# Denominators and pair preparation a group later, the feed-forward queued by token block, the rounding without mid waits, sums of the first batch on VectorE

## The chip, the cores and the metric

The kernel runs on 1 core of one Trainium2 chip. The metric is the device time of one execution in microseconds; the figure for the kernel before is the median of 3 runs. A profile is one further execution, in which the hardware recorded every instruction, wait and DMA. Engines: PE (TensorE: matmuls, with its weight loads listed as PEld), DVE (VectorE), ACT (ScalarE), POOL (GpSimd) and SP (SyncE, which here only issues DMAs). Each engine works through its own instructions in the order in which the program wrote them.

## The reference

Routed attention, then a bilinear feed-forward, all in float32. Batch 4, 8 heads, 768 tokens, head size 64, 16 clusters a head; 3072 tokens of 512 features, 1536 hidden features.

```python
q_assign = np.argmax(np.einsum('bhsd,hcd->bhsc', q_n, c_n), axis=-1)   # normalized q, centroids
k_assign = np.argmax(np.einsum('bhsd,hcd->bhsc', k_n, c_n), axis=-1)
mask = q_assign[:, :, :, None] == k_assign[:, :, None, :]
scores = np.where(mask, scale * np.matmul(q, k.transpose(0, 1, 3, 2)), -1000000000.0)
attn = np.exp(scores - np.max(scores, axis=-1, keepdims=True))
attn = attn / (np.sum(attn, axis=-1, keepdims=True) + 1e-09)
x = np.matmul(attn, v).transpose(0, 2, 1, 3).reshape(B * S, H * D)
out = ((x @ w_a) * (x @ w_b)) @ w_out          # weights passed as float64
```

## The kernel before

The order of instructions on each engine is the order of the program text; nothing is reordered by a scheduler.

*Units, groups, pairs.* Heads are taken in 16 pairs p (4 per batch). A unit is 128 keys (index j, 0 to 5) against half the queries (384, index hf) for both heads of a pair (index a). Two units make a group, 6 groups (GPP) a pair, 96 groups (NG) in all. The main loop (L527) goes over groups g; p, l = divmod(g, 6). The three groups with l = 0, 1, 2 are the first half of a pair's queries, l = 3, 4, 5 the second.

*One turn of the loop.* `score` of group g: 4 one-hot matmuls (L371) put a large negative number where clusters differ, 4 score matmuls (L380) add on top, into one of 2 PSUM buffers `s` per unit, and ScalarE takes the exponentials into `pt` (L387; 4 buffers, two groups). Then `add_up` of group g - 1 (L400): sums of the probabilities over j, elementwise, into `acc`; for a = 1 and for j = 2 and 4 on GpSimd, else on VectorE. Then `weigh` of group g - 1 (L411): probabilities times v into `O`; after the last j ScalarE copies `O` to `xT` (L419). Then one step of the next pair's preparation, then roundings that are due, then feed-forward pieces, then `denominators` and `normalize` where they fall.

*Preparation* of pair p + 1 (`prep_steps`, L343): l=0 transposes of q and k, first third (L275); l=1 the other two thirds and the DMAs of the pair after; l=2 similarities to the centroids (L288) and the DMA of v; l=3 `prep_assign`: transposes (L299) and five VectorE passes that turn maxima into one-hots (L305 to L316); l=5 transposes of the one-hots (L326) and two ScalarE copies (L331, L333).

*Denominators.* At g % 3 == 0 ones are multiplied with `acc` (L427), ScalarE copies the result to `den` and sums it into `stat` (L431). At g % 3 == 1 `normalize` takes three reciprocals on VectorE (L440), GpSimd multiplies `xT` by them (L442), and ScalarE makes a pass over `den` that fills another column of `stat` (L444).

*Feed-forward.* A batch has two blocks of 384 tokens. A block is 24 up pieces (w_a and w_b in turn for 12 slices of hidden features, L458; ScalarE copies the first to `ha`, L469, VectorE multiplies the second into `h`, L473) and 3 down pieces (L479), whose result ScalarE copies to `y` (L483), which SP stores. Pieces wait in the queue `ffn`; a turn may spend PER_GROUP = 4608 columns, an up piece costs 1536 and a down piece 6144. A batch's pieces are queued when its last half is normalized. What is left after the loop runs at the end, behind one piece and a matmul (L572) that checks all denominators; a second path, which runs only if that check fails, is not entered.

*Weights* arrive as float64 in 36 parts of 128x512 (`load_w`, 512 KB each, 2 buffers `raw`) and are rounded to float32 from their bits (`round_w`): on VectorE L222, L225, L229, L232, and L235, which takes the exponent; a sum on GpSimd (L238); and a VectorE pass that sets the tiniest to zero (L240). `due` (L514) gives the group in which a part is rounded: 2, 5, ..., 23 for the first eight, then 1.6 a group from 24. The DMA of part i + 2 follows the rounding of part i on SP.

*Buffers.* PSUM: `s` 2, `O` 1, and 3 buffers `m` for everything else: transposes, similarities, one-hots, denominators, feed-forward pieces. The kernel opens with the centroids' norms on ScalarE and VectorE (L83 to L105) and the whole preparation of pair 0 (L519 to L526).

## Time and profile before

| | us |
|---|---|
| median of 3 runs | 1224.48 (1223.28 to 1226.19) |
| the profiled execution, its own time | 1223.04 |
| its span, first to last instruction | 1221.3 |
| PE busy | 1162.9 |
| DVE / ACT / POOL busy | 413.5 / 317.8 / 326.0 |
| granted TensorE clock, mean | 0.983 |
| first score matmul | 18.1 |
| group 24 (pair 4) begins | 144.6 |
| first feed-forward piece | 160.5 |
| last sums of attention | 1002 |
| last feed-forward matmul ends | 1216 |

The span is what the profile covers, from the first to the last instruction; the run's own time is 1.7 us longer. A busy share is an average over stages, so it is read by stretches. A wait is named by the instruction that waited and by the one that released it; a line number stands for all instructions that one line of the program issues. Slices of the page are 30.5 us each.

### The profile page before, as it was taken

Reading aid. Unit: us, or ns where it says so; the run is one execution under the profiler, and the core shown is the slowest. Engines: PE = TensorE matmul, PEld = TensorE weight load, DVE = VectorE, ACT = ScalarE, POOL = GpSimd, SP = SyncE. Lnnn points to the kernel's source line nnn. Section 1 sums busy time; section 2 is a strip of 40 time slices with the busy share of each in tenths; the row PEclk is TensorE's granted clock in tenths of the full one; section 3 lists DMA queues with packets and bytes.
Section 4 is the critical chain, followed back from the end, with each engine's and each line's share of the span. In section 5 each row is a group of like instructions: output and inputs, shape, how many; then the busy total and the mean of one; then the engine's idle time right before and its main releaser. Section 6 shows DMA issues by size and latency. Waiting matters only on the chain.

```text
span 1221.3 us, 11866 instructions
## 1 busy us (share of the span) xinstructions
PE 1162.9 (95%) x4723; PEld 576.6 (47%) x4723; DVE 413.5 (34%) x602; ACT 317.8 (26%) x575; POOL 326.0 (27%) x301
## 2 busy tenths in 40 slices
PE   6978869999989999999999999999999998999998
PEld 3333335545544445554455544554445544554553
DVE  3777777677671202223112321313022221100100
ACT  4544422222322223322223223222233211000000
POOL 2665643344432212222112222204122220000000
PEclk8998979999999999999999999999999999999999
DMA  4212241412311001010010102010000000000000
GB/s 117 76 56 72 74 125 53 125 52 83 94 35 35 31 18 48 1 39 9 27 31 1 39 13 53 1 39 1 18 22 1 1 9 17 1 1 26 1 1 28
DMA packets 63374, 44.91 MB, mean 37 GB/s; under 512 B 51536, under 2 KB 55632, under 8 KB 63312
## 3 DMA queue, kind: packets, MB, share of 16 engines
q1 hardware_dynamic: 63168, 44.05, 12.6%
q8 instruction: 39, 0.64, 0.2%
q14 instruction: 23, 0.19, 0.1%
q10 hardware_dynamic: 144, 0.03, 0.0%
HBM read 37.78 MB, written 6.29 MB: 36 GB/s over the span
## 4 chain that ended last, share of the span: by engine, by line
PE 80%; DVE 8%; issue 5%; POOL 5%; ACT 1%; DMA 0%; POOLq 0%; DVEq 0%; ACTq 0%
PE m L458 37%; PE m L479 20%; PE O L411 8%; PE s L380 7%; PE s L371 2%; POOL acc L400 2%; DVE den L440 2%; PE m L427 2%; PE m L275 2%; DVE acc L400 2%; POOL wb_sb L238 1%; POOL wa_sb L238 1%; PE m L288 1%; POOL wo_sb L238 1%; DVE rest L232 1%
## 5 line engine op out<-in xcount | busy, mean ns | idle before, releaser
L458 PE MATMUL m<-xT,wa_sb 128*128 128x384 f32 x768 | 268.3, 493 | 13.9 <-ACT sim L293 10.7
L458 PE MATMUL m<-xT,wb_sb 128*128 128x384 f32 x768 | 267.6, 492 | 2.1 <-DVE h L473 2.1
L479 PE MATMUL m<-wo_sb,h 128*128 128x512 f32 x576 | 251.5, 594 | 0.0
L400 POOL TENSOR_TENSOR acc<-acc,pt 128x384 f32<-128x384 f32 x192 | 204.4, 1080 | 52.4 <-ACT pt L387 47.4
L458 PEld LDWEIGHTS m<-xT,wa_sb 128*128 128x128 f32 x768 | 144.9, 192 | 123.5 <-ACT sim L293 11.3
L458 PEld LDWEIGHTS m<-xT,wb_sb 128*128 128x128 f32 x768 | 145.3, 192 | 100.2 <-issue 3.5
L473 DVE TENSOR_TENSOR h<-ha,m 128x384 f32<-128x384 f32 x96 | 52.7, 552 | 368.8 <-PE m L458 368.8
L479 PEld LDWEIGHTS m<-wo_sb,h 128*128 128x128 f32 x576 | 108.0, 190 | 133.5 <-issue 130.6
L387 ACT ACTIVATE pt<-s 128x768 f32<-128x768 f32 x192 | 145.1, 806 | 64.1 <-PE s L380 60.6
L411 PE MATMUL O<-pt,v 128*64 128x384 f32 x768 | 145.8, 501 | 0.0
L469 ACT COPY ha<-m 128x384 f32<-128x384 f32 x96 | 46.0, 480 | 377.7 <-PE m L458 377.5
L380 PE MATMUL s<-qkT 64*128 64x384 f32 x768 | 143.9, 495 | 0.0
L400 POOL TENSOR_TENSOR acc<-pt 128x384 f32<-128x384 f32 x32 | 39.5, 1235 | 353.0 <-PE m L427 333.4
L400 DVE TENSOR_TENSOR acc<-acc,pt 128x384 f32<-128x384 f32 x64 | 74.1, 1157 | 126.7 <-POOL acc L400 126.7
L440 DVE RECIPROCAL den<-den 128x128 f32<-128x128 f32 x96 | 82.3, 913 | 23.4 <-ACT den L431 22.8
L411 PEld LDWEIGHTS O<-pt,v 128*64 128x64 f32 x768 | 46.9, 137 | 88.4 <-issue 87.8
L380 PEld LDWEIGHTS s<-qkT 64*128 64x128 f32 x768 | 72.7, 193 | 33.2 <-issue 3.0
L442 POOL TENSOR_TENSOR xT<-xT,den 128x384 f32<-128x384 f32 x32 | 31.9, 997 | 190.2 <-DVE den L440 188.3
L483 ACT COPY y<-m 128x512 f32<-128x512 f32 x24 | 14.1, 586 | 244.6 <-PE m L479 244.6
L400 DVE TENSOR_TENSOR acc<-pt 128x384 f32<-128x384 f32 x32 | 18.6, 580 | 142.0 <-PE m L427 135.1
L371 PE MATMUL s<-ohT 64*128 64x384 bf16 x384 | 49.3, 336 | 8.8 <-ACT ohT L333 8.8
L427 PE MATMUL m<-acc,ones 128*64 128x384 f32 x128 | 35.5, 528 | 12.2 <-DVE acc L400 12.2
(77 smaller groups left out, 507.2 us busy)
## 6 DMA issues: line engine op xcount, KB each, us to landing
qk<-in_q_dram SPq DMA_DIRECT2D x32, 192.0 KB, 3.6
qk<-in_k_dram SPq DMA_DIRECT2D x32, 192.0 KB, 3.9
v<-in_v_dram SPq DMA_DIRECT2D x16, 384.0 KB, 4.4
raw<-in_moe_w_a_dram SPq DMA_DIRECT2D x12, 512.0 KB, 3.6
raw<-in_moe_w_b_dram SPq DMA_DIRECT2D x12, 512.0 KB, 3.6
raw<-in_moe_w_out_dram SPq DMA_DIRECT2D x12, 512.0 KB, 3.3
out_dram<-y SPq DMA_DIRECT2D x24, 256.0 KB, 2.0
csb<-in_centroids_dram ACTq DMA_DIRECT2D x1, 32.0 KB, 1.8
```

Source lines behind the costliest of these rows:

```text
L238: nc.gpsimd.tensor_tensor(out=w, in0=w, in1=rest, op=ALU.add)
L371: nc.tensor.matmul(out=s[:, a, 0:HB], lhsT=ohTs[p][r, S + j * P:S + (j + 1) * P], rhs=ohTs[p][r, hf * HB:(hf + 1) * HB], start=True, stop= ...
L380: nc.tensor.matmul(out=s[:, a, 0:HB], lhsT=qkTs[p][r, S + j * P:S + (j + 1) * P], rhs=qkTs[p][r, hf * HB:(hf + 1) * HB], start=False, stop ...
L387: nc.scalar.activation(out=pt, in_=s[:, :, 0:HB], func=AF.Exp, scale=SCALE)
L400: eng.tensor_tensor(out=acc[:, a, :], in0=probs[u - 1][:, a, :] if j == 1 else acc[:, a, :], in1=probs[u][:, a, :], op=ALU.add)
L411: nc.tensor.matmul(out=O_of[0][a * D:(a + 1) * D, 0:HB], lhsT=vs[p][:, a, j, :], rhs=probs[u][:, a, :], start=(j == 0), stop=(j == NJ - 1))
L427: nc.tensor.matmul(out=ps[a * D:(a + 1) * D, 0:HB], lhsT=ones, rhs=acc[:, a, :], start=True, stop=True)
L440: nc.vector.reciprocal(out=part, in_=part)
L458: nc.tensor.matmul(out=ps[:, 0:HB], lhsT=w_sb[:, ch, f * P:(f + 1) * P], rhs=xTs[b][:, ch, t0:t0 + HB], start=(ch == 0), stop=(ch == NCH - 1))
L469: nc.scalar.copy(out=box["a"], in_=ps[:, 0:HB])
L473: nc.vector.tensor_tensor(out=box["h"][:, f, :], in0=box["a"], in1=ps[:, 0:HB], op=ALU.mult)
L479: nc.tensor.matmul(out=ps, lhsT=box["h"][:, f, n * P:(n + 1) * P], rhs=wo_sb[:, f, :], start=(f == 0), stop=(f == NF - 1))
```

## The change

At the start, the k loads of pair 0 are issued by ScalarE, the centroids' work becomes a function called behind these loads (the square and its sum on VectorE), the centroid transpose goes behind the query transposes, two of the three transpose copies and one one-hot copy of pair 0 go to VectorE, and the assignment of pair 0 runs in two halves, keys first.

In the loop, all three transposes are in step l=0, similarities in l=1, the assignment in l=2, the one-hots in l=4. Denominators come at g % 3 == 1 and normalizing at g % 3 == 2, a group later than before, and denominators now stand ahead of the turn's roundings and pieces; `acc` has 2 buffers and `y` 1. For the four pairs of the first batch GpSimd keeps the sums with a = 1 and j = 1 or 3 only.

A rounding no longer computes the exponent: ScalarE writes the absolute value of the high word, read as float32, into `size`, and the last VectorE pass compares that. This pass is put off to `flush_w`, which runs ahead of the next rounding or in the next turn behind the sums. Roundings are spread over a turn, one ahead of the pieces and one behind each piece, and are due at 1 + int(2.5 i) for the first eight and 1.5 a group from group 20 on.

A block is queued as soon as its own half is normalized: in the first batch 8 up pieces of block 0, then the two blocks in turns of 8; in the others a block whole. Four pieces instead of one stand ahead of the last check, and the loop has one more turn.

```diff
@@ -25,6 +25,8 @@
+
+SMALLEST = 1.125 * 2.0 ** -15
...
+
+    one = const.tile([P, 1], FP32)
+    nc.vector.memset(one, 1.0)
+    ce = const.tile([P, 1], FP32)
...
-    csq = const.tile([P, D], FP32)
-    cs2 = const.tile([P, 1], FP32)
-    nc.scalar.activation(out=csq, in_=csb, func=AF.Square, accum_out=cs2)
-    cn0 = const.tile([P, 1], FP32)
-    nc.scalar.activation(out=cn0, in_=cs2, func=AF.Sqrt)
...
+    def centroids_in():
+
+        nc.scalar.activation(out=ce, in_=one, func=AF.Sqrt)
+        csq = const.tile([P, D], FP32)
+        cs2 = const.tile([P, 1], FP32)
+        nc.vector.tensor_tensor(out=csq, in0=csb, in1=csb, op=ALU.mult)
+        nc.vector.tensor_reduce(out=cs2, in_=csq, axis=AX.X, op=ALU.add)
+        cn0 = const.tile([P, 1], FP32)
+        nc.scalar.activation(out=cn0, in_=cs2, func=AF.Sqrt)
+
+        nc.scalar.activation(out=ce, in_=cn0, func=AF.Exp)
...
+        nc.vector.tensor_copy(out=rank, in_=rank_i)
+        nc.vector.tensor_copy(out=identb, in_=ident)
...
-    accp = pool("accp", 1)
+    accp = pool("accp", 2)
...
-    yp = pool("yp", 2)
+    yp = pool("yp", 1)
...
         for w, src in enumerate((q, k)):
+            eng = nc.scalar if p == 0 and w == 1 else nc.sync
             for a in range(2):
-                nc.sync.dma_start(
+                eng.dma_start(
                     out=t[:, w, :, a, :],
                     in_=src[b, 2 * hp + a].rearrange("(p j) d -> p j d", j=NJ))
...
     load(0)
+    centroids_in()
     load_v(0)
...
+    flush = []
+
     def round_w(i):
-        if i >= len(w_parts):
-            return
+        flush_w()
         w = w_parts[i][0]
         wi = w.bitcast(INT32)
         raw = raws.pop(i)
...
-        ex = wtp.tile([P, WN], INT32, name="ex")
-        nc.vector.tensor_scalar(out=ex, in0=hi, scalar1=1, scalar2=21,
-                                op0=ALU.logical_shift_left,
-                                op1=ALU.logical_shift_right)
+
+        size = wtp.tile([P, WN], FP32, name="size")
+        nc.scalar.activation(out=size, in_=halves(FP32)[:, :, 1], func=AF.Abs)
         nc.gpsimd.tensor_tensor(out=w, in0=w, in1=rest, op=ALU.add)
-
-        nc.vector.scalar_tensor_tensor(out=w, in0=ex, scalar=897.0, in1=w,
-                                       op0=ALU.is_ge, op1=ALU.mult)
+        flush.append((w, size))
+
+    def flush_w():
+
+        while flush:
+            w, size = flush.pop(0)
+            nc.vector.scalar_tensor_tensor(out=w, in0=size, scalar=SMALLEST,
+                                           in1=w, op0=ALU.is_ge, op1=ALU.mult)
 
...
-    ps = ps_m.tile([P, 512], FP32, name="m")
-    nc.tensor.transpose(out=ps[:, 0:P], in_=cn.rearrange("p a d -> p (a d)"),
-                        identity=ident)
-    nc.vector.tensor_copy(out=cT, in_=ps[:, 0:P])
...
+    def centroids_across():
+        ps = ps_m.tile([P, 512], FP32, name="m")
+        nc.tensor.transpose(out=ps[:, 0:P], in_=cn.rearrange("p a d -> p (a d)"),
+                            identity=ident)
+        nc.vector.tensor_copy(out=cT, in_=ps[:, 0:P])
...
         dst = qkTs[p][:, i * 512:(i + 1) * 512]
-        nc.scalar.copy(out=dst, in_=ps)
+        if p == 0 and i != 1:
+            nc.vector.tensor_copy(out=dst, in_=ps)
+        else:
+            nc.scalar.copy(out=dst, in_=ps)
...
-    def prep_assign(p):
+    def prep_across(p):
         ps = ps_m.tile([P, 512], FP32, name="m")
         for t in range(3):
             nc.tensor.transpose(out=ps[:, t * P:(t + 1) * P],
                                 in_=sims[p][:, t * P:(t + 1) * P],
                                 identity=ident)
+        return ps
+
+    def prep_assign(ps, w=None):
+
+        def of(t, e):
+            if w is None:
+                return t.rearrange("p (n e) -> p n e", e=e)
+            t = t.rearrange("p (t w n e) -> p t w n e", t=3, w=2, e=e)
+            return t[:, :, w]
+
+        def spread(t):
+            t = of(t, 1)
+            return t.broadcast_to(tuple(t.shape[:-1]) + (NC,))
...
     def prep_onehot(p, w):
-        if w == 0:
+        if p not in ohTs:
             ohTs[p] = ohtp.tile([P, 2 * S], BF16, name="ohT")
...
         dst = ohTs[p][:, w * S:(w + 1) * S]
-        if w == 0:
-            nc.scalar.copy(out=dst, in_=ps[:, 0:S])
-        else:
+        if w == 1:
             nc.scalar.activation(out=dst, in_=ps[:, 0:S], func=AF.Identity,
                                  scale=FAR, bias=nfar[:, 0:1])
+        elif p == 0:
+            nc.vector.tensor_copy(out=dst, in_=ps[:, 0:S])
+        else:
+            nc.scalar.copy(out=dst, in_=ps[:, 0:S])
...
         return [
-            lambda: prep_transpose(p, 0),
-            both(lambda: prep_transpose(p, 1), lambda: prep_transpose(p, 2),
+            both(*(lambda i=i: prep_transpose(p, i) for i in range(3)),
                  lambda: load(p + 1)),
             both(lambda: prep_sim(p), lambda: load_v(p)),
-            lambda: prep_assign(p),
+            lambda: prep_assign(prep_across(p)),
             lambda: None,
             both(lambda: prep_onehot(p, 0), lambda: prep_onehot(p, 1)),
+            lambda: None,
         ]
...
         for a in range(2):
-            eng = nc.gpsimd if a == 1 or j in (2, 4) else nc.vector
+            if p < HP:
+                eng = nc.gpsimd if a == 1 and j in (1, 3) else nc.vector
+            else:
+                eng = nc.gpsimd if a == 1 or j in (2, 4) else nc.vector
...
-    def ffn_batch(b):
-        blocks = [ffn_block(b, blk) for blk in range(2)]
-        if b == 0:
+    blocks = {}
+
+    def ffn_ready(b, blk):
+
+        ups, downs = blocks[b, blk] = ffn_block(b, blk)
+        if b > 0:
+            ffn.extend(ups + downs)
+        elif blk == 0:
+            ffn.extend(ups[0:8])
+        else:
+            ups0, downs0 = blocks[b, 0]
             for n in range(3):
-                for ups, _ in blocks:
-                    ffn.extend(ups[8 * n:8 * n + 8])
-            for _, downs in blocks:
-                ffn.extend(downs)
-        else:
-            for ups, downs in blocks:
-                ffn.extend(ups + downs)
+                ffn.extend(ups[8 * n:8 * n + 8] + ups0[8 * n + 8:8 * n + 16])
+            ffn.extend(downs0 + downs)
...
     due = {}
     for i in range(len(w_parts)):
-        due.setdefault(3 * i + 2 if i < 8 else 24 + int((i - 8) / 1.6),
+        due.setdefault(1 + int(2.5 * i) if i < 8 else 20 + int((i - 8) / 1.5),
                        []).append(i)
 
-    prep_transpose(0, 0)
-    prep_transpose(0, 1)
-    prep_transpose(0, 2)
+    for i in range(3):
+        prep_transpose(0, i)
     load(1)
+    centroids_across()
     prep_sim(0)
-    prep_assign(0)
-    prep_onehot(0, 0)
-    prep_onehot(0, 1)
-    for g in range(NG + 2):
+    ps = prep_across(0)
+    for w in (1, 0):
+        prep_assign(ps, w)
+        prep_onehot(0, w)
+    for g in range(NG + 3):
         p, l = divmod(g, GPP)
         if l == 0:
             ready = prep_steps(p + 1)
@@ -535,27 +580,37 @@
         if 0 < g <= NG:
             for u in before:
                 add_up(u)
+        flush_w()
+        if 0 < g <= NG:
             weigh(before)
         if g < NG:
             ready[l]()
-        for i in due.get(g, ()):
-            round_w(i)
-            load_w(i + 2)
+        if g % 3 == 1 and 3 < g:
+            denominators(*divmod(g // 3 - 1, 2))
+        parts = due.get(g, [])
+
+        def round_next():
+            if parts:
+                i = parts.pop(0)
+                round_w(i)
+                load_w(i + 2)
+
+        round_next()
         if ffn:
             credit += PER_GROUP
             while ffn and credit > 0:
                 cost, piece = ffn.popleft()
                 credit -= cost
                 piece()
+                round_next()
         else:
             credit = 0
-        if 0 < g <= NG and g % 3 == 0:
-            denominators(*divmod((g - 1) // 3, 2))
-        if 1 < g <= NG + 1 and g % 3 == 1:
-            ph = divmod((g - 2) // 3, 2)
+        round_next()
+        if g % 3 == 2 and 3 < g:
+            ph = divmod(g // 3 - 1, 2)
             normalize(*ph)
-            if ph[1] == 1 and ph[0] % HP == HP - 1:
-                ffn_batch(ph[0] // HP)
+            if ph[0] % HP == HP - 1:
+                ffn_ready(ph[0] // HP, ph[1])
...
-    ffn.popleft()[1]()
+    for _ in range(4):
+        ffn.popleft()[1]()
```

## The prediction

> **What bounds the kernel now.** I read the page's busy table and slices first, then TensorE's waits up to the feed-forward, busy time by stretches cut at each head pair's first scores, then the timeline where a wait named a queue. Durations are from the one profiled execution: span 1221.3 us, its run 1223.04, so 1.7 lies around the span; the median shown, 1224.48, is 1.4 above that run.
>
> ```profile
> PE 1162.9 (95%) x4723; PEld 576.6 (47%) x4723; DVE 413.5 (34%) x602; ACT 317.8 (26%) x575; POOL 326.0 (27%) x301
> ...
> PE   6978869999989999999999999999999998999998
> ...
> PEclk8998979999999999999999999999999999999999
> ```
>
> TensorE is the bound; all 58 us of its idle time lie in the start, the first batch (slices 2 to 13), the step after the last attention group and the tail. TensorE's waits from 20 to 194 us, its own rows:
>
> ```profile
> PE m L427 <- DVE acc L400: 12.2, 7, 2.4
> PE m L458 <- ACT sim L293: 10.7, 1, 10.7
> PE s L371 <- ACT ohT L333: 7.8, 4, 2.1
> ```
>
> Denominators wait for sums, the feed-forward once, scores for the one-hots. By pairs (span, length, busy of PE, PEld, DVE, ACT, POOL, clock):
>
> ```profile
> 44.99:77.83 32.84, 27.66 (x163) 11.66 (x164) 23.93 (x30) 15.89 (x28) 20.43 (x18) 0.95 0.26 69
> 77.83:111.39 33.56, 27.49 (x163) 11.73 (x163) 24.63 (x30) 15.89 (x28) 20.27 (x18) 0.95 0.25 67
> 111.39:144.62 33.23, 27.32 (x165) 11.63 (x165) 23.62 (x30) 15.78 (x28) 20.44 (x18) 0.95 0.26 68
> 144.62:181.99 37.37, 25.98 (x110) 11.96 (x110) 27.69 (x41) 8.62 (x16) 17.98 (x16) 0.77 0.40 108
> ```
>
> From later undisturbed groups a bare group takes 3.16 us of TensorE; a pair adds transposes 1.42, similarities 0.78, L299 0.39, one-hots 0.70, two denominators 1.6: 6 x 3.16 + 4.9 = 23.9. So each pair loses 9 us: 5.2 idle, the rest at a lower clock.
>
> ScalarE's queue is what the change meets most. Timeline of steady groups (start, length):
>
> ```profile
> 679.10 0.55 DVE L473 TENSOR_TENSOR h<-ha,m 128x384 f32<-128x384 f32 x1 [4.61 <-PE m L458]
> 679.57 2.57 DVE L440 RECIPROCAL den<-den 128x128 f32<-128x128 f32 x3
> 682.28 1.00 POOL L442 TENSOR_TENSOR xT<-xT,den 128x384 f32<-128x384 f32 x1 [13.73 <-DVE den L440]
> 683.32 0.52 ACT L444 ACTIVATE den<-den 128x384 f32<-128x384 f32 x1 [6.39 <-POOL xT L442]
> 683.84 1.49 ACT L387 ACTIVATE pt<-s 128x768 f32<-128x768 f32 x2
> 685.22 0.48 ACT L293 COPY sim<-m 128x384 f32<-128x384 f32 x1
> ```
>
> Normalizing ends in a ScalarE pass (L444) that waits for reciprocals and GpSimd's product; the next exponentials stand behind it. Here the group began at 678.93 and its exponentials 4.9 us later, not 0.95.
>
> **The change, part by part.** Below, l is the group's place in its pair, T(l) its first score.
>
> *Start.* Two key loads move to ScalarE's DMA queue (2 x 0.65 of issue before its first table load), the centroid chain goes behind them, two copies go to VectorE, the assignment is halved. Before: similarities end at 11.3, assignment 3.06, one-hots and copies to 18.11. After, the centroid transpose and its copies (0.29 + 0.39) stand behind the query transposes and eat what the earlier ones save; the second half of the assignment, 1.6, runs beside the first half's 0.91 copy. I take 0.4 gained (bounds: 3 lost if the keys land late, 2 gained). The first scores are at 17.7.
>
> *Denominators, preparation, normalizing, in pairs without feed-forward.* One group later the sums are ready and the one-hot copies have a group of cover: both waits go (about 5 us a pair). But assignment and one normalizing now share group l=2. L299 runs 3.16 after T(2), assignment starts at 3.75, takes 2.98, reciprocals 2.6, product and L444 1.75: exponentials of l=3 start at T(2)+11.1, and the next scores, which need the score buffer back (+0.9), at 12.0, where PE alone would be at 6.7. That wait is 5.3, plus some 2 for the clock (half of the 3.8 that a pair lost by three waits). A pair: 23.9 + 5.3 + 2 = 31.2; 2.3 more where a rounding stands between (pair 1); pair 0 has none of it, 24.
>
> *Rounding.* 36 tests on VectorE (0.42 each) become 36 absolute values on ScalarE; no row has one, so I bound it by 128x512 copies, 0.59, and the 0.8 of an exponential, and take 0.6. ScalarE is 48% busy there (15.9 of 32.8), so this hides; without that cover it would cost 0.6 x 14 = 8. VectorE's four instructions take 2.3; the last (0.69) waits for GpSimd's sum (1.39) only when the next rounding follows at once. With one `size` buffer ScalarE also waits there, with the exponentials behind it.
>
> *Sums on VectorE.* Per pair GpSimd goes from 14 sums of 1.0 to 4, VectorE from 6 of 0.55 to 16. A VectorE instruction behind a GpSimd one waits it out (L222: 0.42 alone, 1.22 beside sums). With two products (2.0) and the assignment's two-operand passes (1.1), shared work falls from 20.4 to 15.9 a pair, and from 4.7 to 4.3 a rounding.
>
> *Group 20 on.* Before reached group 20 at 128.2 with 6 roundings done; after: 17.7 + 24 + 33.5 + 31.2 + 9.3 = 115.7, with 8. But six more are due in groups 20 to 23, ahead of the normalizing on which the feed-forward now starts. VectorE from T(20): 3.75 until L299, assignment 3.0, six roundings 13.8, two waits for GpSimd inside a group 4.4, other closings 2.1, eight sums 4.4, six reciprocals 5.2, waits behind GpSimd 5.8: 42.5. The product ends at 44.1; L444, exponentials and the first transpose copy (all three `m` buffers are taken) let the first piece in at 46.6. Then group 24 7.7 + 2.6 clock (the piece at 176.56 took 5.49), group 25 4.7 + 7.7, group 26: assignment, two roundings, product at +17.8, and four pieces 10.3 + 1.8 clock: group 28 at 115.7 + 99.2 = 214.9. Before had it at 194.26 with 6 pieces fewer (x 2.58 = 15.5): 209.8. **Lost: 5.1.** Bounds: 8 more if the absolute values find no cover, 18 less in the rival below.
>
> *Rest of the rounding.* Before lost 10.4 from there to 400 us (idle 8.6, clock 1.8), mostly products behind a rounding; interleaving them by piece ends that. **Gained: 10.4**, less 2 x 2.8 from the next part.
>
> *Three transposes in one group.* They take all three `m` buffers at l=0. Where l=5 ended in a piece of w_b, the rows above put the ScalarE copies at T+6.3; xT (0.48) goes first, so the first buffer is free at 7.4, while PE is through at 4.6: 2.8 us idle. By the credits, three pieces a group, this falls on groups 30, 36, 54, 66, 78, 90. The first two stand above; the other four lie where before had no idle at all. **Lost: 4 x 2.8 = 11.2** (bounds 0, and 18 with a cold piece each time). The Trainium skill ("TensorE: Matmul & The Clock Gate", Part 1) drops the clock only after an idle window of about 3.4 us; the row at 260.40 shows 2.10 idle and then 4.54 for a piece of 2.74. By the page nothing is added here; by that row up to 4 x 1.8, and I leave it to the range.
>
> *End.* Half a batch queues early and four pieces precede the last check: the 3.15 us wait at 1031 and its cold piece (4.54 for 2.74) go. **Gained: 5.0.** What hides it is the queued first block; if that ran dry, 5 would return.
>
> *At nothing:* the loads of the next pair stand one group earlier on SP behind the transposes (landing 3.6 to 3.9, with over four groups of 3.2 to spare; otherwise 3.9 a pair); weight loads must now also await ScalarE's pass; one `y` buffer (a store lands in 2.0, downs are 10.3 apart; were they not, 2 each); the second `acc` buffer.
>
> Sum: 5.1 - 10.4 + 5.6 + 11.2 - 5.0 = +6.5; span 1227.8, run 1229.5, median 1230.9, say **1231**.
>
> **Rivals.** *The shared work decides* (faster). Before, 18.1 to 194.3 held 4 x 20.4 + 13.6 + 15 x 4.73 = 166 us of it, 94% of 176. After, to the same group with 20 roundings: 63.6 + 13.6 + 86 = 163; at 94%, 174 from 17.7 gives 191, 18.5 ahead of 209.8 in place of 5.1 behind: 1231 - 23.6 = 1207. For it: that 94%. Against: ScalarE's wait at l=2 holds PE whatever GpSimd does. It decides once the 46.6 from group 20 to the first piece is under 40.
>
> *The buffer wait is not there* (faster, slightly): if transposes are copied before the exponentials matter, 11.2 falls away: 1220. Against: the 3.23 us wait of L458 at 365 is the same chain.
>
> *Absolute value needs another table* (far slower). Two loads of 1.28 a rounding on ScalarE, 14 of them before the feed-forward: 36 us, 1266. For: the page's L83 load for a square, followed by another for the root. Against: copies and exponentials share a table in every row.
>
> The Trainium skill ("ScalarE: Activation LUTs", Table sets) lists abs as filler of every set; no run here shows it, and by it this rival would be empty.
>
> *The change does nothing*: excluded by moved rows, though sums may cancel.
>
> **How the numbers follow.** Forecast 0.47 at 1231, its own range 1224 to 1241; shared work 0.30; no buffer wait 0.16; table 0.04; other cancelling 0.03. A measurement tells 0.2%, about 2.4 us. Faster: 0.28 of the shared-work case, 0.11 of the next, 0.04 of the forecast's edge: 0.43. Same: 0.09. Slower: 0.48. The range leaves out the table and the fast third of the shared-work case: 1204 to 1241.
>
> **What would show it.** Right: L458 waiting for ACT qkT (2 to 3 us) at groups 54, 66, 78, 90; exponentials of l=3 waiting for L444; the first L458 near 162 us; no wait of L427 for sums or of L371 for one-hots; none at the last check. Wrong: the first L458 before 145 us, 100% busy from 450 to 1000, or table loads between exponentials.

## The result, and the profile after

The changed kernel takes 1233.11 us (median of 4 runs, 1232.8 to 1233.68); the kernel before took 1225.34 beside it (4 runs, 1223.28 to 1226.79). The ratio is 1.0065, 95% interval 1.0048 to 1.0083: slower, by 7.8 us. The span of the profiled execution is 1231.1, 9.8 more than before. The page of the changed kernel, busy times and two rows of slices (30.8 us each):

```profile
PE 1160.1 (94%) x4723; PEld 578.6 (47%) x4723; DVE 404.5 (33%) x617; ACT 331.4 (27%) x606; POOL 275.7 (22%) x261
...
PE   5978578999999999999999999999999999999998
...
PEclk9988889999999999999999999999999999999999
```

TensorE is busy for 2.8 us less than before and idle for 12.6 more. GpSimd has lost 50 us of work, and the time is longer all the same. TensorE's waits say why:

```profile
PE s L409 <- ACT pt L425: 27.9, 10, 11.6
PE m L499 <- ACT qkT L301: 22.1, 6, 9.0
...
PE m L499 <- POOL xT L483: 3.2, 1, 3.2
```

The columns are total, number, longest. The waits of before, for sums (12.2), for the late feed-forward (10.7) and for one-hots (7.8), are gone in this form (the 0.6 for one-hots that is left stands at the first score). In their place stand 50 us of waits for ScalarE, of two kinds: scores whose PSUM buffer the exponentials have not read, and feed-forward pieces whose buffer `m` the transposes' copies have not read. Of the 22.1, 9.0 falls on the first feed-forward piece, so the feed-forward is still held up; 13.1 falls on five later groups. Stretches: the pairs 1, 2 and 3, then groups 24 to 26 (columns: span, length, busy time of PE, PEld, DVE, ACT and POOL with the number of instructions, granted clock, DMA share, GB/s):

```profile
42.68:78.50 35.82, 27.02 (x165) 11.96 (x164) 29.01 (x46) 17.15 (x32) 12.36 (x10) 0.86 0.23 63
78.50:109.78 31.28, 26.15 (x165) 11.62 (x164) 25.73 (x37) 16.59 (x31) 10.37 (x8) 0.89 0.29 75
109.78:149.58 39.80, 26.11 (x165) 11.66 (x164) 31.63 (x52) 18.27 (x34) 12.17 (x10) 0.87 0.36 107
149.58:195.63 46.05, 36.73 (x152) 19.11 (x152) 28.25 (x47) 13.45 (x25) 12.87 (x11) 0.89 0.30 83
```

*First kind.* Timeline of pair 2 (start, length, engine, line; in brackets the idle time before and what ended it). Group l=2 began at 87.87:

```profile
88.55 0.66 ACT L249 ACTIVATE size<-raw 128x512 f32<-128x512 f32 x1
...
91.03 0.55 PE L320 MATMUL m<-ident,sim 128*128 128x128 f32 x3
91.51 0.50 PE L409 MATMUL s<-ohT 64*128 64x384 bf16 x4
91.61 0.56 DVE L341 TENSOR_REDUCE mx<-m 128x24 f32<-128x384 f32 x1 [1.61 <-PE m L320]
...
94.45 2.57 DVE L481 RECIPROCAL den<-den 128x128 f32<-128x128 f32 x3
...
97.16 1.11 POOL L483 TENSOR_TENSOR xT<-xT,den 128x384 f32<-128x384 f32 x1 [7.86 <-DVE den L481]
98.31 0.52 ACT L485 ACTIVATE den<-den 128x384 f32<-128x384 f32 x1 [7.68 <-POOL xT L483]
...
98.83 1.49 ACT L425 ACTIVATE pt<-s 128x768 f32<-128x768 f32 x2
99.67 0.51 PE L409 MATMUL s<-ohT 64*128 64x384 bf16 x2 [4.93 <-ACT pt L425]
```

Assignment, reciprocals, product and the second pass over `den` follow each other, and the exponentials of l=3 stand behind the pass on ScalarE: they start at T(2)+11.0, and the scores of l=4 stand still until T(2)+11.8. In pairs 1, 2 and 3 this wait is 7.26, 4.93 and 11.57.

*Second kind.* Timeline at group 54 (l=0), in the steady part that had no idle at all before:

```profile
526.13 2.74 PE L499 MATMUL m<-xT,wb_sb 128*128 128x384 f32 x8
...
528.98 0.55 DVE L514 TENSOR_TENSOR h<-ha,m 128x384 f32<-128x384 f32 x1 [4.61 <-PE m L499]
...
529.45 2.57 DVE L481 RECIPROCAL den<-den 128x128 f32<-128x128 f32 x3
...
531.96 1.53 PE L293 MATMUL m<-ident,qk 128*128 128x128 f32 x12
532.16 1.00 POOL L483 TENSOR_TENSOR xT<-xT,den 128x384 f32<-128x384 f32 x1 [21.96 <-DVE den L481]
...
533.20 0.52 ACT L485 ACTIVATE den<-den 128x384 f32<-128x384 f32 x1 [6.39 <-POOL xT L483]
...
533.72 1.49 ACT L425 ACTIVATE pt<-s 128x768 f32<-128x768 f32 x2
...
535.10 0.48 ACT L460 COPY xT<-O 128x384 f32<-128x384 f32 x1
535.46 1.58 ACT L301 COPY qkT<-m 128x512 f32<-128x512 f32 x3
536.12 4.28 PE L499 MATMUL m<-xT,wa_sb 128*128 128x384 f32 x8 [2.63 <-ACT qkT L301]
```

The group before ended in a piece of w_b, whose product (L514) holds VectorE until 529.45. So the reciprocals end late, the pass too, behind it the exponentials, the copy of `O` and the three copies that would free a buffer. TensorE waits 2.63, and its next piece takes 4.28 where 2.85 is usual: the group is 16.96 long, not 12.43. The same stands at groups 30, 36, 66 and 78.

Where the 9.8 us of span come from: group 0 begins at 19.79 (before 18.11); group 28 at 212.78, with six pieces more behind it (6 x 2.58), so 3.0 late, the start's 1.7 included. The buffer waits at groups 30 and 36 cost 4.5 + 2.8, those at 54, 66 and 78 13.6. The end gives back 5.0: nothing waits at the last check. The rest, -9.1, is found by subtraction; before had lost 10.4 between group 28 and 400 us (8.6 in waits, 1.8 in one slow piece), and nothing of that kind is left.

### The profile page after: what moved, and what is told of

The parts are those of the page before. It is cut to its first block, busy times and chain, and to the rows that moved or that the text cites. A ratio compares the mean times of both kernels' runs of the same rounds, so it can differ in the third digit from the quotient of the medians.

```text
span 1231.1 us, 11821 instructions
## 1 busy us (share of the span) xinstructions
PE 1160.1 (94%) x4723; PEld 578.6 (47%) x4723; DVE 404.5 (33%) x617; ACT 331.4 (27%) x606; POOL 275.7 (22%) x261
## 4 chain that ended last, share of the span: by engine, by line
PE 83%; DVE 5%; ACT 2%; POOL 1%; issue 1%; DVEq 0%; POOLq 0%; ACTq 0%
PE m L499 41%; PE m L520 20%; PE O L452 8%; PE s L418 7%; PE s L409 2%; DVE den L481 2%; PE m L468 2%; ACT pt L425 1%; PE m L309 1%; PE m L362 1%; PE m L293 1%; POOL xT L483 1%; PE m L320 0%; DVE rest L245 0%; DVE acc L441 0%
## 5 line engine op out<-in xcount | busy, mean ns | idle before, releaser
L499 PE MATMUL m<-xT,wa_sb 128*128 128x384 f32 x768 | 274.4, 502 | 25.3 <-ACT qkT L301 22.1
L441 POOL TENSOR_TENSOR acc<-acc,pt 128x384 f32<-128x384 f32 x152 | 157.7, 1051 | 248.1 <-ACT pt L425 238.8
L514 DVE TENSOR_TENSOR h<-ha,m 128x384 f32<-128x384 f32 x96 | 53.1, 554 | 476.8 <-PE m L499 476.8
L441 DVE TENSOR_TENSOR acc<-acc,pt 128x384 f32<-128x384 f32 x104 | 89.5, 890 | 188.4 <-POOL acc L441 185.9
L409 PE MATMUL s<-ohT 64*128 64x384 bf16 x384 | 50.3, 334 | 28.6 <-ACT pt L425 27.9
L409 PEld LDWEIGHTS <-ohT 64*128 64x128 bf16 x384 | 12.1, 94 | 84.5 <-issue 80.2
L441 POOL TENSOR_TENSOR acc<-pt 128x384 f32<-128x384 f32 x32 | 36.9, 1154 | 61.9 <-ACT pt L425 61.9
L485 ACT ACTIVATE den<-den 128x384 f32<-128x384 f32 x32 | 16.8, 524 | 93.8 <-POOL xT L483 93.8
```

The costliest lines, as they stand in the source:

```text
L409: nc.tensor.matmul(out=s[:, a, 0:HB], lhsT=ohTs[p][r, S + j * P:S + (j + 1) * P], rhs=ohTs[p][r, hf * HB:(hf + 1) * HB], start=True, stop= ...
L441: eng.tensor_tensor(out=acc[:, a, :], in0=probs[u - 1][:, a, :] if j == 1 else acc[:, a, :], in1=probs[u][:, a, :], op=ALU.add)
L499: nc.tensor.matmul(out=ps[:, 0:HB], lhsT=w_sb[:, ch, f * P:(f + 1) * P], rhs=xTs[b][:, ch, t0:t0 + HB], start=(ch == 0), stop=(ch == NCH - 1))
L514: nc.vector.tensor_tensor(out=box["h"][:, f, :], in0=box["a"], in1=ps[:, 0:HB], op=ALU.mult)
```

## The experiments

All are edits of the changed kernel (1233.1). The expectations speak of "waits of l=3": these are the waits of the first kind, which TensorE meets in the scores of the next group. Medians, with the ratio to the kernel before, measured beside it:

| run | edit | us | ratio, 95% interval |
|---|---|---|---|
| e1_pass_behind | second pass over `den` behind the next exponentials | 1212.77 | 0.9892 [0.9875, 0.9909] |
| e2_split_assign3 | transposes over two groups, assignment at l=3 | 1200.04 | 0.9782 [0.9759, 0.9805] |
| e3_assign3_only | assignment at l=3 alone | 1222.03 | 0.9974 [0.9963, 0.9984] |
| e4_due24 | roundings due later | 1215.48 | 0.9916 [0.9899, 0.9932] |
| e5_keys_sp | first keys on SP's queue again | 1230.93 | 1.0053 [1.0033, 1.0072] |
| e6_sums_undone | sums as before | 1243.10 | 1.0144 [1.0113, 1.0175] |
| e7_rounding_undone | rounding as before | 1250.79 | 1.0209 [1.0181, 1.0236] |
| e8_end_undone | batches 1 to 3 queued whole, one piece before the check | 1222.20 | 0.9992 [0.9973, 1.0011] |
| e11_denominators_undone | denominators and normalizing where they were | 1199.81 | 0.9795 [0.9769, 0.9821] |
| e12_shift_undone_late | e11, roundings later, keys on SP | 1181.67 | 0.9638 [0.9625, 0.9652] |
| e10_three | e2, e4 and e5 together | 1178.14 | 0.9618 [0.9593, 0.9644] |
| e9_all_four | e10 and e1 together | 1177.88 | 0.9609 [0.9582, 0.9636] |

### The pass ahead of the exponentials (e1)

```diff
-        nc.scalar.activation(out=den, in_=den, func=AF.Copy,
-                             accum_out=stat[:, n:n + 1])
+        late.append(lambda: nc.scalar.activation(
+            out=den, in_=den, func=AF.Copy, accum_out=stat[:, n:n + 1]))
...
         if g < NG:
             score(now)
+        while late:
+            late.pop(0)()
```

> The changed kernel, but ScalarE's second pass over den (L485) is issued behind the next group's exponentials instead of ahead of them. Theory (ScalarE's queue order makes both the wait at l=3 and the buffer wait at l=0): the five waits of L499 for the transpose copies go with their cold pieces (5 x 2.6 + some 8 of clock = 21 us); the waits at l=3 of pairs 1 to 3 (7.3, 4.9, 11.6) shrink only in part, since VectorE's sums then come late for the exponentials of l=4 (perhaps 6 us gained). About 1206 us. Rival (the shared work of VectorE and GpSimd sets the first batch, and the steady waits come from the three transposes alone): no change in either place, 1233.

Measured: 20.3 less than the change, 6.8 short of the theory and far from the rival. The waits of this kernel:

```profile
PE m L501 <- ACT qkT L301: 12.2, 6, 6.1
PE s L409 <- ACT pt L425: 11.8, 4, 5.8
PE O L452 <- ACT xT L460: 9.9, 3, 5.2
```

The order on ScalarE's queue is the cause of much of both kinds. But the pass still waits for the product, only now with the copies of `O` and of the transposes behind it: the buffer waits shrink from 2.63 to 1.23 and the first kind turns into a wait for the copy of `O`. This profile's start is also 2.3 later than the change's (first score 22.08), which e5 takes up.

### Assignment and transposes (e2, e3)

```diff
-            both(*(lambda i=i: prep_transpose(p, i) for i in range(3)),
+            lambda: prep_transpose(p, 0),
+            both(lambda: prep_transpose(p, 1), lambda: prep_transpose(p, 2),
                  lambda: load(p + 1)),
             both(lambda: prep_sim(p), lambda: load_v(p)),
             lambda: prep_assign(prep_across(p)),
-            lambda: None,
             both(lambda: prep_onehot(p, 0), lambda: prep_onehot(p, 1)),
             lambda: None,
```

In the change each step of the preparation stands a group earlier than before (the title of this document says later). This is e2, which gets the assignment away from the normalizing and splits the transposes. e3 keeps the three transposes at l=0 and moves the assignment alone:

```diff
             both(lambda: prep_sim(p), lambda: load_v(p)),
-            lambda: prep_assign(prep_across(p)),
             lambda: None,
+            lambda: prep_assign(prep_across(p)),
             both(lambda: prep_onehot(p, 0), lambda: prep_onehot(p, 1)),
```

> The changed kernel with the preparation spread again: one transpose at l=0, two at l=1, similarities at l=2, the assignment at l=3 (away from the normalizing at l=2), one-hots still at l=4. Theory: buffer waits gone (21 us), the waits at l=3 of pairs 1 and 2 gone (12 us and some 3 of clock), group 20 some 3 us shorter: about 1197. Rival (shared work decides the first batch): only the 21 of the later groups, 1212.

> The changed kernel with the assignment alone moved from l=2 to l=3; three transposes stay at l=0. Theory: the waits at l=3 of pairs 1 and 2 go (15 with clock), the five buffer waits stay: about 1217. Rival (shared work): within 3 of 1233.

Measured: e3 gains 11 us, e2 33, each some 3 to 5 less than its theory. TensorE at group 54, where the preparation of pair 10 begins, in e3, in which nothing has changed there:

```profile
519.87 1.53 PE L293 MATMUL m<-ident,qk 128*128 128x128 f32 x12
524.03 4.54 PE L499 MATMUL m<-xT,wa_sb 128*128 128x384 f32 x8 [2.63 <-ACT qkT L301]
```

and in e2:

```profile
513.73 0.66 PE L293 MATMUL m<-ident,qk 128*128 128x128 f32 x4
514.23 2.75 PE L499 MATMUL m<-xT,wa_sb 128*128 128x384 f32 x8
```

One transpose instead of three leaves two buffers `m` free; the piece starts at once and at the full clock. The 22 us between e3 and e2 are for the most part the five buffer waits with their slow pieces (20.9 in the change). The 11 of e3 are the meeting of assignment and normalizing in l=2: the waits of 7.26, 4.93 and 11.57 become 2.80, 1.19 and 5.45.

### Roundings later (e4)

```diff
-        due.setdefault(1 + int(2.5 * i) if i < 8 else 20 + int((i - 8) / 1.5),
+        due.setdefault(1 + int(2.5 * i) if i < 8 else 24 + int((i - 8) / 1.7),
```

> The changed kernel with the roundings of parts 8 to 35 due from group 24 on at 1.7 a group instead of from group 20 at 1.5. Theory (six roundings ahead of the first feed-forward piece hold it back): the first piece starts near 146 us instead of 163.8, some 4 of this are given back while rounding runs beside the feed-forward: about 1220. Rival (the total of shared work decides, wherever it is put): 1233, with the waits moved into groups 24 to 40.

Measured: 17.6 gained, 4.5 more than expected. The wait of group 22's scores falls from 11.57 to 5.01, and the first feed-forward piece, at 148.35, no longer waits 8.96 for a buffer. So the six roundings due in groups 20 to 23 did hold the feed-forward back; they are not needed that early.

### The parts undone (e5 to e8, e11)

```diff
-            eng = nc.scalar if p == 0 and w == 1 else nc.sync
+            eng = nc.sync
```

> Changed kernel (1233.1) with one word undone: the first pair's keys go out on SP's queue again, behind the queries; the centroid chain and the halved assignment stay. Theory: the 1.7 us by which the first score is late (19.79 against 18.11) is the keys' landing, 5.1 us after issue from ScalarE's queue against 3.9 from SP's; the first score comes at 18.6 or earlier and the time is 1231.5 (1230.5 to 1232.5). Rival: the centroid transpose and copies that now stand behind the query transposes cost it; the first score stays at 19.5 to 20 and the time at 1233 (1 either way).

Measured: 2.2 gained, and the first score at 18.34, as the theory had it. But it is not the keys alone. TensorE's first rows in the change:

```profile
6.17 1.51 PE L293 MATMUL m<-ident,qk 128*128 128x128 f32 x6 [6.17 <-DMA qk<-in_q_dram]
8.24 1.51 PE L293 MATMUL m<-ident,qk 128*128 128x128 f32 x6 [0.55 <-DMA qk<-in_k_dram]
```

and here:

```profile
5.25 3.06 PE L293 MATMUL m<-ident,qk 128*128 128x128 f32 x12 [5.25 <-DMA qk<-in_q_dram]
```

With the keys on a second queue the queries, issued first and at the same time as here (0.80), land 0.9 us later. The Trainium skill ("DMA: Bandwidth & Descriptors", "Issuing engines are not separate DMA queues") says that transfers of all issuing engines interleave on the same 16 DMA engines, and that a second issuer saves issue time only. The later queries agree with that. What was saved, an issue of the keys at 1.23 in place of 2.20, was lost again in their landing.

```diff
-            if p < HP:
-                eng = nc.gpsimd if a == 1 and j in (1, 3) else nc.vector
-            else:
-                eng = nc.gpsimd if a == 1 or j in (2, 4) else nc.vector
+            eng = nc.gpsimd if a == 1 or j in (2, 4) else nc.vector
```

> Changed kernel with the sums of the first batch split as before: 14 a pair on GpSimd, 6 on VectorE. Theory: until group 20 TensorE waits for ScalarE's queue, whose head waits for VectorE's assignment and reciprocals; taking 5.5 us of sums a pair off VectorE and putting 10 on GpSimd moves that little, the product gets later by a sum or two (1 to 2 us a pair): 1236 (1233 to 1241). Rival, the one of the prediction: the work that VectorE and GpSimd share decides; it grows by 4.5 us in each of four pairs and by 0.4 a rounding: 1233 + 18 + 8 = 1259, and not under 1249.

Measured: 10.0 lost, between the two: neither range held it. Until group 22 the waits grow by 0.1, 1.7 and 0.1 (7.35, 6.66, 11.67); then that of group 24, at 154.28, is 3.58 in place of 1.80, and by 252.61 the kernel is 8.7 behind the change, 5.8 of it lost between groups 22 and 30, beside the roundings. So the shared work doesn't decide, but the new split of the sums is worth 10 us.

```diff
-        size = wtp.tile([P, WN], FP32, name="size")
-        nc.scalar.activation(out=size, in_=halves(FP32)[:, :, 1], func=AF.Abs)
+        ex = wtp.tile([P, WN], INT32, name="ex")
+        nc.vector.tensor_scalar(out=ex, in0=hi, scalar1=1, scalar2=21,
...
         nc.gpsimd.tensor_tensor(out=w, in0=w, in1=rest, op=ALU.add)
-        flush.append((w, size))
+        nc.vector.scalar_tensor_tensor(out=w, in0=ex, scalar=897.0, in1=w,
+                                       op0=ALU.is_ge, op1=ALU.mult)
```

> Changed kernel with the rounding as before: the exponent test on VectorE in place of the absolute value on ScalarE, and the last VectorE instruction right behind GpSimd's sum, so it waits for it in the middle. When a rounding is queued (by group, and between pieces) stays as in the change. Theory: VectorE is the bound only in groups 20 to 26, where six to ten roundings stand ahead of the normalizing that the feed-forward waits for: 8 x (0.42 + 1.2 of waiting) = 13, less some 5 of waits for the single size buffer on ScalarE; the first feed-forward piece comes at 170 to 174 in place of 163.8 and the time is 1241 (1236 to 1248). Rival: VectorE binds in the whole of the rounding, 36 x 1.6 = 58 less what TensorE's queue covers: over 1255. Second rival: the wait in the middle is hidden, 1233 (2 either way).

Measured: 17.7 lost, more than the theory's range. The keys landed late in this profile (first score 22.70, 2.9 behind the change's); the first feed-forward piece is at 175.38, 8.7 behind besides, and group 30's piece at 260.27, 13.5 behind. The profiled execution is 20.6 longer than the change's; without the 2.9 of the keys that is 17.7 too. So the new rounding is worth some 18 us in the change, most of it up to group 30. Which of its two parts earns it, the exponent test on ScalarE or the pass that no longer waits in the middle, is not shown, since both were undone together.

```diff
         if b > 0:
-            ffn.extend(ups + downs)
+            if blk == 1:
+                for u, d in (blocks[b, 0], blocks[b, 1]):
+                    ffn.extend(u + d)
...
-    for _ in range(4):
-        ffn.popleft()[1]()
+    ffn.popleft()[1]()
```

> Changed kernel with the end as before: the second batch's two token blocks are queued together after the last normalizing, and one piece, not four, precedes the last check. Theory: the wait that stood at the last check before comes back, 3.2 us idle and 1.8 for the cold piece behind it: 1238 (1236 to 1240). Rival: with normalizing a group later there is more to wait for, nothing is queued in the groups behind the last attention group: 1244 or more. Second rival: the 5.0 that the end gained came from elsewhere: 1233 (1 either way).

Measured: 10.9 **gained**, where all three theories had none. Two things show in the trace. First, the three buffer waits of groups 54, 66 and 78 are gone. With a batch queued whole, its pieces begin three groups later (group 51, not 48); nine pieces are an odd number, so now l=5 ends in a piece of w_a. Timeline at this kernel's group 54:

```profile
502.44 0.56 DVE L514 TENSOR_TENSOR h<-ha,m 128x384 f32<-128x384 f32 x1 [7.50 <-PE m L499]
502.91 2.57 DVE L481 RECIPROCAL den<-den 128x128 f32<-128x128 f32 x3
504.84 0.50 PE L409 MATMUL s<-ohT 64*128 64x384 bf16 x4
...
508.00 1.53 PE L293 MATMUL m<-ident,qk 128*128 128x128 f32 x12
508.55 0.48 ACT L460 COPY xT<-O 128x384 f32<-128x384 f32 x1
508.91 1.58 ACT L301 COPY qkT<-m 128x512 f32<-128x512 f32 x3
...
509.57 2.85 PE L499 MATMUL m<-xT,wb_sb 128*128 128x384 f32 x8
```

The reciprocals start 1.93 ahead of the group's scores; in the change they start 0.65 behind them, and that is the whole wait. Second, the wait at the last check doesn't come back:

```profile
1016.72 10.57 PE L520 MATMUL m<-wo_sb,h 128*128 128x512 f32 x24
...
1017.53 2.58 DVE L481 RECIPROCAL den<-den 128x128 f32<-128x128 f32 x3 [20.06 <-ACT den L472]
...
1020.26 0.99 POOL L483 TENSOR_TENSOR xT<-xT,den 128x384 f32<-128x384 f32 x1 [21.93 <-DVE den L481]
...
1027.85 0.53 ACT L485 ACTIVATE den<-den 128x384 f32<-128x384 f32 x1
...
1028.98 0.15 DVE L625 TENSOR_SCALAR far_off<-least 128x1 f32<-128x1 f32 x1
...
1029.80 0.19 PE L629 MATMUL m<-ones,far_off 128*1 128x1 f32 x2
```

The batch was queued a group later than before, since normalizing is, so one down piece of 10.57 is left for the turn after the last attention group and stands between the denominators and the check. The end's 5.0 is covered by this alone, without the early queue and the four pieces.

```diff
-        if g % 3 == 1 and 3 < g:
-            denominators(*divmod(g // 3 - 1, 2))
...
-        if g % 3 == 2 and 3 < g:
-            ph = divmod(g // 3 - 1, 2)
+        if 0 < g <= NG and g % 3 == 0:
+            denominators(*divmod((g - 1) // 3, 2))
+        if 1 < g <= NG + 1 and g % 3 == 1:
+            ph = divmod((g - 2) // 3, 2)
```

> Changed kernel with the denominators and the normalizing back where they were before: denominators behind the feed-forward of the third group of a half, normalizing a group later (l=1 and l=4 in place of l=2 and l=5). Preparation, feed-forward queue, rounding and sums stay as in the change. Theory: both stalls of the change come from normalizing in the group right ahead of what they hold up, so with it at l=1 and l=4 the buffer waits at l=0 (20.9 with their cold pieces) and the long waits of l=3 (23.8, of which some 5 stay as shorter waits elsewhere) go, while denominators wait for their sums again (12 in seven waits before, fewer now that VectorE makes most sums: 6 to 12, and half as much for the clock): 1233 - 21 - 19 + 14 = 1207 (1200 to 1218); TensorE waits for sums at l=0 and l=3. Rival: the shift is what the change lives on, the stalls come from the assignment at l=2 and from three transposes in a group wherever the normalizing is: 1233 + 14 = 1247, not under 1235.

Measured: 33.3 gained, just under the theory's range (1200 to 1218). Assignment at l=2 and three transposes at l=0 stay, yet:

```profile
PE m L468 <- DVE acc L441: 17.7, 4, 8.8
...
PE m L499 <- POOL xT L483: 3.5, 1, 3.5
PE s L409 <- ACT pt L425: 3.2, 3, 2.5
```

The waits of 27.9 and 22.1 for ScalarE have shrunk to 3.2 and none. But sums are waited for again, four times, each at l=3, where in pairs 1 to 3 of the change the exponentials were late. The longest, of pairs 1 and 3:

```profile
69.32 2.01 PE L468 MATMUL m<-acc,ones 128*64 128x384 f32 x4 [5.45 <-DVE acc L441]
...
132.15 2.01 PE L468 MATMUL m<-acc,ones 128*64 128x384 f32 x4 [8.76 <-DVE acc L441]
```

Group 24 begins at 156.36, behind three pieces that the change has not yet run there (7.7), so at 148.6 against 149.6: up to there the two are level. Some 14 us are gained between groups 24 and 28, where the first pieces had waited, and 20.9 are the buffer waits. Of these the run doesn't show that normalizing at l=4 removes them, because the feed-forward starts a group earlier as well and l=5 now ends in a piece of w_a, as in e8. The first piece behind the transposes of group 54 is one of w_b:

```profile
517.41 2.81 PE L499 MATMUL m<-xT,wb_sb 128*128 128x384 f32 x8
```

So the shift by a group, the first item of the change, costs 33 us together with what it meets in this kernel. It is not the only way to win them back: e2 keeps the shift and gains as much. The rest of the change without the shift is 2% faster than before.

### Is the shift worth anything? (e12), and the best kernels (e9, e10)

e12 joins e11 with e5 and with roundings due from group 23, 1.7 a group. e10 keeps the shift and has e2, e4 and e5; e9 has e1 too.

> The kernel with denominators and normalizing back (1199.8), with the roundings due from group 23 at 1.7 a group and the first keys on SP's queue; assignment at l=2 and three transposes in a group stay as in the change. Question: whether the shift by a group is worth anything once its stalls are taken away by other means (the kernel with the shift, spread transposes, assignment at l=3 and later roundings ran at 1178.1). Theory: in the kernel at 1199.8 TensorE waited 17.7 for sums, 8.8 of it at group 21 and 3.5 more at group 24, both behind roundings; later roundings take those two and their clock (half as much again), and the keys 1.5: 1199.8 - 18 - 1.5 = 1180 (1176 to 1186), so the shift is worth nothing over its absence, within 6. Rival: the sums' waits of every pair stay with the clock they cost, 17.7 less 8.8, half as much again and one-hots on top: 1192 or more, so the shift is worth 14 once the stalls are gone.

> Changed kernel with three edits: transposes over two groups and assignment at l=3, roundings due from group 24 at 1.7 a group, first keys on SP's queue; the second pass stays where the change has it. Theory: 1200 - 8 - 2 = 1190 (1185 to 1196). Rival: the waits of groups 20 to 24 were what held the roundings back in time, and roundings that come later run into the feed-forward's own pieces: no faster than 1200 less the 2 of the keys, 1198 (2 either way).

> Changed kernel with four edits together: one head pair's transposes over two groups and the assignment at l=3 (1200.0 alone), the roundings due from group 24 at 1.7 a group (1215.5 alone, 17.6 less than the change), the first keys on SP's queue (2.2 less), and the denominators' second pass behind the next exponentials (1212.8 alone, 20.3 less). The edits overlap: the first takes all buffer waits and most of l=3's, so of the pass only l=3's rest is left (some 4 to 8), and of the later roundings the waits in groups 20 to 24, 3.7 + 5.65 + 4.44 in that kernel, say 8. Theory: 1200 - 8 - 2 - 5 = 1185 (1180 to 1191), faster than the same without the moved pass by 3 to 6. Rival: with the transposes spread, the moved pass stands ahead of the transposes' copies and of the attention output's copy on ScalarE and gives back what it saves: equal to the kernel without it within 2.

Measured: 1181.67, 1178.14 and 1177.88. e12 met its theory; in it TensorE waits 10.9 for sums. e10 came out under its range (1185 to 1196) and e9 too: the later roundings were worth more than the 8 that I gave them: against e2, TensorE's waits for the exponentials fall from 19.9 to 9.2, and the 3.7 for the product of the first piece goes. e9 against e10 met the rival: the moved pass gains nothing once the stalls are gone. The page of e10:

```profile
PE 1147.4 (98%) x4723; PEld 572.4 (49%) x4723; DVE 410.3 (35%) x617; ACT 332.7 (28%) x606; POOL 273.6 (23%) x261
...
PE   6898999999999999999999999999999999999998
```

e10, with the shift and its stalls removed, is 3.5 us under e12, without it; their intervals overlap, e12's roundings begin a group earlier, and its preparation is the change's. Whether the shift itself is worth anything is therefore not shown. e9 and e10 are the fastest kernels found, 3.8% to 3.9% under the kernel before.

## Why the prediction was right, and where it wasn't

The forecast, 1231 and slower, held by its main step and met the time within 2.1 us. That it came so close is partly luck, since the terms err both ways: -2.1 up to group 28, +1.7 at groups 30 and 36, +2.4 at the later buffer waits, +1.3 in the rest of the rounding. Point by point:

- *The meeting at l=2* (predicted: exponentials of l=3 at T(2)+11.1, a wait of 5.3, a pair of 31.2): 11.0, 4.93 and 31.28 in pair 2. e3 shows the cause: with the assignment a group later, the wait is 1.19. In e11, with the normalizing a group earlier, the exponentials are waited for no more, but sums are, at the same place.
- *Three transposes in one group* (predicted 4 x 2.8 at groups 54, 66, 78, 90 and two earlier): right mechanism, wrong count and size. There is no wait at 90, since pair 15 is the last and has no successor to prepare; and each of the steady waits costs 4.5, since the piece behind it runs slowly, which I had left to the range. 13.6 in place of 11.2. "They take all three `m` buffers" is one condition, and the piece that ends l=5 another: e2 (one transpose) and e8 (a piece of w_a at the end of l=5) each remove the wait. The place of the normalizing is a third by the timeline, but not shown alone: e11 changes it and the piece together.
- *Start* ("0.4 gained"): 1.7 lost. My bound of keys that land late was the fact; e5 shows that the second queue delays the queries as well; without it the start is still 0.2 later than before, so the rest of the start's work gained nothing.
- *Group 20 on* ("Lost: 5.1" up to group 28): 3.0. The parts erred both ways: group 20 came at 119.4, not 115.7, and the first piece 44.3 after it, not 46.6. In the comparison there, before's 128.2 is the start of its group 21 (group 20 is at 124.3); the sum didn't use it.
- *Rounding.* The absolute value takes 0.66 to 0.73 (taken: 0.6), and the trace has no table load behind the two of the start. I priced the whole part by its cover and gave it no gain of its own; e7 shows some 18. It was inside the comparison with 194.26 all the same, so the sum was not wrong by it.
- *End* ("what hides it is the queued first block"): the 5.0 is right, and in the change pieces of the first block do stand ahead of the check. "If that ran dry, 5 would return" is wrong: in e8 no first block is queued, and the down piece that the later queue leaves over hides the check as well.
- *Rivals.* "The shared work decides" falls with e6: it is worth 10 us, not 26. "The buffer wait is not there" falls with the waits list. "Another table" falls with the 0.66 row and the missing table loads.

What I did not see is the balance between the parts. I charged the stalls to assignment and transposes; e11 shows that with the normalizing back in its old place neither bites, though the first batch gets no shorter by it. Sums and rounding, 10 and some 18 us when undone in the change, are together about what e11 gains on the kernel before (26 us); that they earn it there was not measured.

## What to carry to other kernels

A step moved to another slot of a steady loop is to be checked against what already sits in that slot, by engine queue: here a normalizing pass landed behind an assignment in one slot and ahead of buffer-freeing copies in another, and 27% busy on ScalarE said nothing of it. Queue phase matters too: which of two alternating pieces ends a group decided over 4.5 us at every second pair, so an edit that only shifts when a queue fills can cost or save 1% far from its place. And a part that removes visible waits (here for sums, 12 us) is to be undone alone once the whole is measured: it lost 33 us as it stood, and three other parts, the preparation a group earlier (33), the early roundings (18) and the feed-forward queued by block (11), each lost as well; these figures overlap.

## What the runs showed of the hardware

- Behind a TensorE idle of 2.62 to 2.63 us the next piece took 4.28 to 4.54 us at four of the five buffer waits in the change, but 2.85 at 319.72, the usual time. The clock records say why. The granted clock is half over one stretch of 3.41 us (537.38 to 540.80 behind the wait at 536.12: 0.50) and full at 319.72, and in each of the 14 profiles such stretches start whole multiples of 3.41 us apart. In the stretch of this grid ahead of the slow piece at 536.12 TensorE was idle for 2.15 us; at 319.72 the idle time is cut by a grid line into 1.83 and 0.79. From 30 us to the last matmuls, all 80 full-clock stretches with 2.05 us or more of idle time were followed by one at half clock, and of 90 with 0.8 to 1.94 us none was.
- The Trainium skill ("TensorE: Matmul & The Clock Gate", Part 1) gives an idle window of some 3.4 us, free-running, before the clock drops. The grid agrees with a free-running window; but the window needed not be idle throughout, 2.05 us in it were enough.
- The first keys on ScalarE's queue land at different times from run to run: in nine profiles with them there, TensorE waited 0 to 3.25 us for them beyond the queries, and began its query transposes at 6.09 to 6.65; in the four with them on SP's queue it waited 0 to 0.39, and began at 5.01 to 5.54.
